# A two-stage attention and mixing kernel: list scheduling by remaining path, one-bank PSUM tiles, and loads gated on earlier loads

## The chip, the cores and the metric

The kernel runs on one core of one Trainium2 chip. The metric is device time in microseconds (us). A core has TensorE (matmuls into the accumulator memory PSUM, which the kernel uses in pieces called banks), VectorE, ScalarE (activation functions by table), GpSimd and SyncE. In the profile they are PE, DVE, ACT, POOL and SP; PEld is TensorE's loading of weights. In this kernel GpSimd issues all loads from HBM (they cast fp32 to bf16 on the way), and SyncE issues the stores, copies of V inside on-chip memory, and transposes done by DMA.

A run more than 1.5% above the fastest of its kernel is called slow; comparisons below use fast runs, each against runs of the kernel before on the same chip.

## The reference, cut to what matters

```python
scores = scale * q @ k.T + bias          # B, H, S, D = 4, 8, 768, 64
# kept: the first 8 positions, and the last 96 up to the query itself
a = softmax(scores);  x = (a @ v)        # heads joined: x is (4, 768, 512)
theta = x @ w_theta                      # 512 x 512
y = w_tok_r @ (x * cos(theta)) + w_tok_i @ (x * sin(theta))    # 768 x 768, over the sequence
u = x + y
out = u + relu(u @ w_ch)                 # 512 x 512
```

Each batch needs all its attention, then theta, then the mix over all positions, so batches overlap: while TensorE mixes one batch, the attention of the next goes in between.

## The kernel before

The kernel is written as a list of operations with a rough duration each. A list scheduler inside the kernel's Python, `Plan`, puts them in an order per engine; the engines then run strictly in that order. So a wrong idea of when data arrives is built into the instruction stream. What the change and the argument touch:

```python
bufs = dict(qk=5, qT=3, kk=3, e=8, x=8, xT=3, ..., w_nat=6, big=2, small=4)   # buffers per pool

def load(fn, nbytes, ndesc, reads=(), writes=(), alloc=None):      # GpSimd issues, in one fixed order
    add(f"load{nload[0]}", {"POOL": 0.62 + 0.00028 * ndesc}, fn, ..., prio=-100 + nload[0],
        lat=(1.5, nbytes / 360e3), after=[previous load])

def load_w_tok(tt):                        # two blocks of 128 rows in one load; 6 loads, 6 buffers
    nc.gpsimd.dma_start(out=w2, in_=src[tt * T:(tt + 2) * T, :].rearrange("(a p) s -> p a s", p=T))

# batches 1 to 3: "vprev", a copy of V shifted by one block, issued by SyncE when V has landed
nc.sync.dma_start(out=dst[NG:T], in_=src[NG:T])
# batches 1 to 3: x transposed by DMA, issued by SyncE too
nc.sync.dma_start_transpose(out=xT, in_=x)
...
big.tile([T, 2, 512], FP)                  # 2 tiles of two PSUM banks: scores of two heads, theta
small.tile(shape, dtype)                   # 4 tiles of one bank: everything else
nc.scalar.activation(e_[:, :, 0:n], tiles[pb][...], AF.Exp, scale=scale)     # both heads at once
...
mix(b, tt, 20 * b + 25, ...)               # priorities are written by hand
```

The softmax here doesn't subtract the row's maximum and nothing guards it: scores larger than these inputs give would overflow.

## Time and profile before

| what | value |
|---|---|
| time, median of 3 | 203.71 us (203.26 to 205.56) |
| span of the profiled run | 200.8 us |
| TensorE busy | 168.4 us, 84% |
| VectorE, ScalarE busy | 124.7, 92.4 us |
| TensorE idle from 70 to 100 us | 16.1 us |
| DMA transpose of x, issue to landing | 8.5 us median, 3.2 at its quickest |

The rows called busy tenths cut the span into 40 slices; a digit is the busy share of a slice in tenths. PEclk is TensorE's granted clock. A line of waits reads: engine, what it was about to write, source line, then what it waited for; total us, times, longest.

### The profile page before, as it was taken

The numbers are of one execution on the slowest core, as the hardware profiler recorded it, in microseconds if no ns is written. First come the engines' busy times: TensorE is split into PE (matmuls) and PEld (weight loads), VectorE is DVE, ScalarE is ACT, GpSimd is POOL, SyncE is SP. The second block draws the span as 40 slices with busy tenths as digits, with TensorE's granted clock in tenths as the row PEclk, the third lists the DMA queues.
The fourth block names the chain that finished last, engine by engine and source line by source line (L and its number), as shares of the span: only waits on it lengthen the run. The fifth ranks groups of instructions, "written<-read, shape, count | busy, mean of one in ns | idle before, by whom it ended". The sixth has DMA issues, their size and how long they took to land.

```text
span 200.8 us, 3765 instructions
## 1 busy us (share of the span) xinstructions
PE 168.4 (84%) x1532; PEld 88.5 (44%) x1532; DVE 124.7 (62%) x243; ACT 92.4 (46%) x100; POOL 69.4 (35%) x85
## 2 busy tenths in 40 slices
PE   7589999899589906804999799999999998999982
PEld 2355466555245502401364355547454653444430
DVE  5475994958496920700397788677988775634351
ACT  2038758899355400600487464187764609400010
POOL 7999745479686855720072000000000000000000
PEclk9859999999999975965899999999999999999998
DMA  5999999999999999999799442832114466124432
GB/s 37 133 147 152 187 210 208 176 154 161 152 184 182 185 138 199 145 148 201 118 102 169 91 131 66 177 100 65 54 30 106 103 148 116 52 52 140 126 104 104
DMA packets 101224, 26.37 MB, mean 131 GB/s; under 512 B 94351, under 2 KB 97055, under 8 KB 101207
## 3 DMA queue, kind: packets, MB, share of 16 engines
q0 software_dynamic: 77568, 12.85, 90.5%
q1 hardware_dynamic: 23639, 13.28, 28.9%
q8 instruction: 12, 0.20, 0.4%
q14 instruction: 5, 0.04, 0.1%
HBM read 25.69 MB, written 6.29 MB: 159 GB/s over the span
## 4 chain that ended last, share of the span: by engine, by line
PE 47%; DMA 33%; POOL 10%; DVE 4%; issue 2%; ACT 1%; SPq 1%; POOLq 0%
PE ps L534 24%; DMA qk<-in_k_dram 11%; PE ps L573 8%; DMA xT<-x 7%; POOL qk L256 6%; PE pb L492 5%; DMA w_nat<-in_moe_w_tok_i_dram 5%; DMA vn<-in_v_dram 5%; DMA out_dram<-o 4%; POOL vn L269 4%; PE pb L448 3%; PE pb L401 3%; DMA uT<-u 2%; PE ps L338 2%; DVE kk L348 1%
## 5 line engine op out<-in xcount | busy, mean ns | idle before, releaser
L534 PE MATMUL ps<-zri,w_tokT 128*128 128x512 bf16 x288 | 70.3, 381 | 0.4 <-ACT w_tokT L327 0.4
L418 ACT ACTIVATE e<-pb 128x1024 bf16<-128x1024 f32 (+1 forms) x48 | 43.9, 951 | 36.3 <-PE pb L401 36.0
L492 PE MATMUL pb<-w_theta_bf,xT 128*128 128x512 bf16 x96 | 25.7, 416 | 16.7 <-DMA xT<-x 16.7
L534 PEld LDWEIGHTS <-w_tokT 128*128 128x128 bf16 x288 | 26.2, 98 | 28.7 <-issue 1.4
L545 DVE TENSOR_TENSOR u<-x,ps 128x512 bf16<-128x512 bf16 x24 | 16.4, 685 | 32.3 <-PE ps L534 32.2
L256 POOL DMA_DIRECT2D qk<-in_q_dram x24 | 21.3, 894 | 25.7 <-PE ps L338 14.7
L426 DVE TENSOR_TENSOR e<-e,etab 128x1024 bf16<-128x1024 bf16 (+1 forms) x36 | 23.0, 642 | 6.7 <-ACT e L418 6.4
L573 PE MATMUL ps<-w_ch_bf,uT 128*128 128x512 bf16 x96 | 24.7, 379 | 1.8 <-DMA uT<-u 1.1
L256 POOL DMA_DIRECT2D qk<-in_k_dram x24 | 21.2, 892 | 5.7 <-DMA qk<-in_q_dram 2.3
L269 POOL DMA_DIRECT2D vn<-in_v_dram x24 | 21.2, 907 | 5.5 <-DMA qk<-in_k_dram 2.0
L492 PEld LDWEIGHTS <-xT 128*128 128x128 bf16 x96 | 9.5, 105 | 30.1 <-DMA xT<-x 18.3
L580 DVE SCALAR_TENSOR_TENSOR o<-ps,u 128x512 f32<-128x512 f32 x24 | 16.6, 690 | 10.0 <-PE ps L573 9.8
L505 ACT ACTIVATE cs<-pb,halfpi 128x1024 bf16<-128x1024 f32 x12 | 13.4, 1114 | 17.5 <-PE pb L492 17.4
L513 DVE TENSOR_TENSOR zri<-x,cs 128x1024 bf16<-128x1024 bf16 x24 | 16.3, 686 | 5.3 <-ACT cs L505 4.8
L338 PE MATMUL ps<-ident,qk 128*128 128x128 bf16 x192 | 15.6, 230 | 4.7 <-DMA qk<-in_q_dram 2.4
L348 DVE COPY kk<-ps 128x2048 bf16<-128x2048 bf16 x12 | 14.5, 1220 | 4.9 <-PE ps L338 4.9
L401 PE MATMUL pb<-qT,kk 64*128 64x128 bf16 x352 | 17.0, 223 | 0.4 <-DVE rec L460 0.4
L401 PEld LDWEIGHTS <-kk 64*128 64x128 bf16 x352 | 10.2, 96 | 14.4 <-issue 12.0
L338 PEld LDWEIGHTS <-qk 128*128 128x128 bf16 x192 | 12.4, 102 | 8.7 <-DMA qk<-in_q_dram 3.4
L505 ACT ACT_TABLE_LOAD x4 | 5.1, 1283 | 23.5 <-PE pb L492 23.5
L448 PEld LDWEIGHTS <-e 128*128 128x128 bf16 x352 | 13.3, 97 | 5.2 <-issue 1.4
L573 PEld LDWEIGHTS <-uT 128*128 128x128 bf16 x96 | 8.5, 98 | 10.8 <-DMA uT<-u 1.7
(53 smaller groups left out, 146.7 us busy)
## 6 DMA issues: line engine op xcount, KB each, us to landing
out_dram<-o SPq DMA_DIRECT2D x24, 256.0 KB, 2.3
qk<-in_q_dram POOLq DMA_DIRECT2D x24, 128.0 KB, 8.3
qk<-in_k_dram POOLq DMA_DIRECT2D x24, 128.0 KB, 8.3
vn<-in_v_dram POOLq DMA_DIRECT2D x24, 128.0 KB, 8.4
vp<-vn SPq DMA_DIRECT2D x9, 243.8 KB, 8.2
w_nat<-in_moe_w_tok_r_dram POOLq DMA_DIRECT2D x3, 384.0 KB, 11.0
w_nat<-in_moe_w_tok_i_dram POOLq DMA_DIRECT2D x3, 384.0 KB, 11.7
w_theta_bf<-in_moe_w_theta_dram POOLq DMA_DIRECT2D x1, 512.0 KB, 6.9
```

The lines of the kernel that those rows point to most:

```text
L256: nc.gpsimd.dma_start(out=tiles["qk", b, g][:, i, t].rearrange("p (h d) -> p h d", d=D), in_=(q, k)[i][b, :, r0:r0 + T, :].rearrange("h p ...
L269: nc.gpsimd.dma_start(out=v_bufs[i][:, t, :, 0:D], in_=v[b, :, r0:r0 + T, :].rearrange("h p d -> p h d"))
L338: nc.tensor.transpose(p_[:, p, t * T:(t + 1) * T], src[:, i, t, p * T:(p + 1) * T], ident)
L401: nc.tensor.matmul(p_[:, hh, s * T:(s + 1) * T], lhsT=tiles["kk", b, kg][R, p, kt, r, :], rhs=tiles["qT", b, g][R, p, qt * T:(qt + 1) * T] ...
L418: nc.scalar.activation(e_[:, :, 0:n], tiles[pb][:, :, 0:n * T].rearrange("p a (s n) -> p a s n", n=T), AF.Exp, scale=scale)
L426: nc.vector.tensor_mul(e_[:, :, 0:n], e_[:, :, 0:n], etab[:, 2 * p:2 * p + 2, s0:s0 + n])
L448: nc.tensor.matmul(o, lhsT=l_, rhs=r_, start=(i == 0), stop=(i == len(mms) - 1))
L492: nc.tensor.matmul(p_[:, t, :], lhsT=tiles["xT", b, g][:, p, t, :], rhs=w_theta_bf[:, p, :], start=(p == 0), stop=(p == NP - 1))
L505: nc.scalar.activation(c_[:, 0], tiles[pb], AF.Sin, bias=halfpi)
L534: nc.tensor.matmul(p_, lhsT=w_tokT[wi][:, 2 * g + t, tt * T:(tt + 1) * T], rhs=tiles["z", b, g][:, wi, t, :], start=(g == 0 and t == 0 and ...
L573: nc.tensor.matmul(p_, lhsT=tiles["uT", b, tt][:, p, :], rhs=w_ch_bf[:, p, :], start=(p == 0), stop=(p == NP - 1))
L580: nc.vector.scalar_tensor_tensor(o_, in0=tiles[ps], scalar=0.0, in1=tiles[uk], op0=ALU.max, op1=ALU.add)
```

## The change

Its intent: let priorities follow from the longest path still ahead, use PSUM in finer pieces, and stop GpSimd's loads of later batches from crowding out SyncE's transfers, by issuing a load only when an earlier one has landed. Cut to its core:

```diff
+    def rank(self):                       # priority: longest remaining path
+        for o in reversed(self.ops):
+            own = min(o.eng.values()) * o.weight
+            tail[o] = own + max((tail[n] + l + ... for n, l in succ.get(o, ())), default=0.0)
...
-    bufs = dict(qk=5, ..., cs=2, ..., w_nat=6, big=2, small=4)
+    bufs = dict(qk=4, ..., cs=3, ..., w_nat=8, pa=4, pb=4)
...
+        if depth:
+            add(f"gate{n}", {"POOL": 0.1},
+                lambda: nc.gpsimd.tensor_copy(out=scrap, in_=landed[n - depth]()),
+                reads=[("ld", n - depth)], prio=-100 + n - 0.5, after=after)
...
-                nc.gpsimd.dma_start(out=w2, in_=src[tt * T:(tt + 2) * T, :]...)      # 6 loads
+                out=new(key, "w_nat", [T, S], BF), in_=src[tt * T:(tt + 1) * T, :])  # 12 loads
...
     for b in range(1, B):
+        depth = 3 if b == 1 else 2
...
-            nc.scalar.activation(e_[:, :, 0:n], tiles[pb][...], AF.Exp, scale=scale)
+            nc.scalar.activation(tiles[ek][:, hh, 0:n], tiles[pb[hh]][:, 0:n], AF.Exp, scale=scale)
...
-            attention(b + 1)
+            plan.weight = 2.0
+            attention(b + 1)
+            plan.weight = 1.0
```

A gate is a copy of one element by GpSimd out of the tile that load n - depth fills. GpSimd works in order, so load n is not issued before that load has landed: at most `depth` loads are in flight. Sines, normalisations and theta are cut to one-bank pieces like the exps; the table of biases for batches 1 to 3 moves to the start. In the profiles of before, `pb` is a two-bank tile and `ps` a one-bank tile; after, `pa` and `pb` are two pools of four one-bank tiles each.

## The prediction

> **What bounds the kernel now.** I read the page first, then the waits, then the chain in order of time, then busy time in stretches of 10 us. The page, sums by engine and the rows of the 40 slices:
>
> ```profile
> PE 168.4 (84%) x1532; PEld 88.5 (44%) x1532; DVE 124.7 (62%) x243; ACT 92.4 (46%) x100; POOL 69.4 (35%) x85
> ...
> PE   7589999899589906804999799999999998999982
> ...
> PEclk9859999999999975965899999999999999999998
> DMA  5999999999999999999799442832114466124432
> ```
>
> TensorE (PE) works 84% of a 200.8 us span, and from slice 21 on it is nearly full. There is one hole, at slices 15 to 20 (some 70 to 100 us), where its clock is cut as well, and a smaller one at slice 11. The DMA engines are near full for as long as loads are issued. The waits name the hole:
>
> ```profile
> PE pb L492 <- DMA xT<-x: 16.7, 4, 8.4
> ...
> POOL qk L256 <- PE ps L338: 14.7, 1, 14.7
> ```
>
> L492 is the theta matmul of batch 1; it waits for xT, a transpose by DMA that SyncE issues. The chain tells why xT is late:
>
> ```profile
> 47.09 7.93 DMA qk<-in_k_dram
> ...
> 69.14 8.52 DMA out_dram<-o
> ...
> 78.63 9.07 DMA vn<-in_v_dram
> ...
> 89.62 8.52 DMA xT<-x
> ...
> 98.18 1.90 PE pb L492 x8
> ...
> 172.43 6.91 PE ps L534 x32
> ```
>
> Every transfer in this stage takes 8 to 9 us, whoever issued it. The xT issue at 89.6 even stands behind copies of V for batch 2 (SyncE issues in order) that waited for a V load to land. The last line is a unit price: 32 matmuls of 512 columns in 6.91 us, 0.216 us each. The stretches:
>
> ```profile
> 50.00:60.00 10.00, 6.62 (x73) 3.55 (x71) 6.88 (x14) 4.36 (x6) 7.51 (x9) 1.00 2.43 169
> ...
> 70.00:80.00 10.00, 2.74 (x7) 1.02 (x8) 1.62 (x4) 0.00 (x0) 5.90 (x7) 0.66 1.87 171
> 80.00:90.00 10.00, 4.62 (x38) 2.27 (x36) 3.85 (x7) 3.31 (x3) 5.26 (x6) 0.84 2.59 148
> 90.00:100.00 10.00, 6.51 (x22) 2.46 (x23) 1.89 (x3) 2.03 (x2) 0.00 (x0) 0.65 1.28 164
> ```
>
> First number: TensorE's busy time in the 10 us. Idle in 70 to 100: 7.26 + 5.38 + 3.49 = 16.1 us. Slow on top of it: eight theta matmuls took 3.59 us at 93.0 and 3.20 us at 77.3, against 1.73 us later, so 3.3 us. At 50 to 60 another 3.4 us go to loads of q and k. The hole is thus worth about 19.5 us. From 100 to 197 TensorE idles only some 3 us.
>
> **What the Trainium skill says.** "DMA: Bandwidth & Descriptors", section "Queues, rings and completion order": each DMA engine goes round the queues that have work, a packet at a time, so GpSimd's and SyncE's transfers slow one another. The trace agrees: xT lands after 8.5 us in the median while loads run and 3.2 us at its quickest; a qk load takes 3.3 us at its quickest (after the pause of 14.7 us) and 8.3 us in the median. "TensorE: Matmul & The Clock Gate", "What's actually happening": an idle window of some 3.4 us halves the clock. It agrees: 0.65 granted in 90 to 100, 0.449 us a matmul against 0.216. "ScalarE: Activation LUTs", "What ACT_TABLE_LOAD costs": an ACTIVATE costs 186 ns + 0.833 ns a column, and neighbours overlap by some 93 ns. The trace has 1022 ns for 1024 columns (formula 1039). For 512 columns I estimate 0.61 us busy, 0.52 from start to start. "PSUM — Partial Sum Buffer", "The four PSUM rules": a matmul's output fits one bank; so a two-bank tile is two matmul groups anyway and can be cut without more matmuls. The built programs agree: as many TensorE instructions in both.
>
> **The change, part by part.**
>
> 1. TensorE's work is unchanged, its order is not. Unit prices from the chain: 512 columns 0.216 us; 24 transposes 1.35 us; 8 score matmuls 0.33; 16 value matmuls 0.48. Per batch: 72 mix, 24 theta, 24 channel matmuls = 120 x 0.216 = 25.9; 48 transposes 2.7; scores 3.7; values 2.7: 35 us. Four batches 140; batch 0's bias matmuls 4.8 (24, about 0.2 each), the other transposes 7, warm-up 3.6: about 155 us if warm and never idle. The 168.4 of before contain 13 us of cold clock and waiting inside groups. Biasing batch 0 on TensorE is nothing new: before had the same 24 bias matmuls.
>
> 2. The exp table (8 x 0.725, some 5.2 us from start to start) moves from 41.8 us, between batch 0 and batch 1, to before the first exp, where ScalarE idles 9.9 us. No table load goes away: 8 in both. Smaller steps: theta in one-bank halves, theta before the transposes of the token weights, those interleaved with the mix. Batch 0's sines should end near 35 us instead of 38.7. But batch 1's q and k cannot arrive sooner, so most of these 4 us turn into a wait for loads.
>
> 3. Gated loads, three in flight for batch 1 and two later. At 3.3 to 3.6 us for a nearly lone load and about 0.3 for gate and semaphore, three in flight give one load per 1.3 us, two give one per 1.9. Before ran one per 1.0 to 1.3. The weights still land near 38 us; batch 1's last k is the 16th load: 39.5 + 15 x 1.3 = 59 us, where before had it at 55.0. So the gate costs 2 to 4 us at the small hole. In return xT, the V copies and stores should land in 3 to 5 us instead of 8.5, and in the new order xT issues no longer queue behind V copies that wait: the hole of 19.5 us shrinks to about 3 (xT of the last group of batch 1: five 0.86 us pieces stand between its values and its theta, against normalise 1 + issue 1.3 + landing 3 to 4).
>
> 4. More small instructions. ScalarE: 32 exps of 1024 columns become 64 of 512, 32 x (2 x 0.61 - 1.022) = +6.3 us; 16 of 768 become 32 of 384 (0.506 each by the same formula), +3.3; 24 cosines and sines become 48 halves, 24 x 0.2 = +4.8; some evacuations (three of q at 1.0, two or three more) leave it, -5. Some 102 us, on an engine with half its time to spare. VectorE: 18 normalisations of two head pairs (0.691 + 0.203) become 36 of one (0.425 + 0.197): 22.4 - 16.1 = +6.3 us; q's evacuations, of which ScalarE did two in batches 2 and 3, go to VectorE almost all: +2. VectorE to about 133 us. Attention of the next batch has double weight, hence is packed tighter: from its first transpose to its last values the new order holds 9.1 us of attention, 11 mix groups and 6 theta or channel groups (17 x 0.863 = 14.7), 23.8 us of TensorE; beside it stand on VectorE 3 k (1.15), 3 q (0.6), 12 multiplications (6.7), 12 normalisations (0.56 each), and nine z, u, o (0.6): 24.7 us. VectorE becomes the tighter engine there, I say 27 us with gaps: +3 us in batch 2 and +3 in batch 3. The 44 matmul groups after batch 3's values are TensorE's alone.
>
> Sum, in span: batch 1's last transpose of k at 59.5. TensorE's work behind it: rest of batch 1's attention 3.3, theta 5.2, rest of mix 0 with channels, and weights 11, mix and channel 1 20.7, batches 2 and 3 70: 110 us, so 169.5 at full pace. Plus 3 (xT), 2 (z behind the last sines of batch 1), 6 (VectorE), 1.5 for the rest; then the end, as before, about 4.5 us from the last mix through u's transposition to the last store. That is 186.5. I take off 3.5, by judgement, because VectorE catches up while TensorE waits for xT or z, so these terms overlap: 183. The time was 1.8 us above the span in the profiled run: **185 us**.
>
> **Rivals.**
>
> A. Two loads in flight starve batches 2 and 3. For: SyncE's transfers keep the engines busy about half the time, and a load that shares takes 4 to 5 us, thus 2.2 to 2.5 us per load; 18 need 40 to 45 us against the 35 us of a batch. Against: a batch's need comes in the middle of its stage, and batch 3 has time. It would cost 5 to 12 us: 190 to 196.
>
> B. VectorE binds throughout attention, with in-order waits, each stage 30 us or longer. For: 24.7 against 23.8 us. Against: it had spare time in every stage of before. 188 to 193.
>
> C. The schedule of the program fits the chip better than I think; no waits for z or xT, loads as early as before. Then 155 us of work, some 10 us of idle start and 5 of end: 172 to 178. For: the new order keeps four or five mix or theta groups between most producers and consumers.
>
> D. The hole stays, since xT still shares with loads and lands in 8 us: 197 to 204. Against: only two or three loads are in flight, where before had five to eight.
>
> **Range and chances.** Most of the 19.5 us must come back unless D holds; A and B take parts of it. A and B together end at 195, C near 177: range 177 to 195. Faster by over 2% (under 199.6): 0.91. Within 2%: 0.07. Slower: 0.02.
>
> **What would show it.** xT's landing in the median at 3 to 5 us; TensorE idle under 10 us in all from 60 us to the last mix, no clock below 0.9 there; busy sum 157 to 162; VectorE 130 to 136; ScalarE 98 to 106; the gates waiting for most of 38 to 130 us on GpSimd; batch 1's last k near 59. Wrong if TensorE waits over 5 us for qk in batch 2 (A), if waits on L462 or on the multiplied e add up to over 10 us (B), or if xT's wait stays over 10 us (D).

## The result, and the profile after

The changed kernel took 223.62 us (median of 3, 221.5 to 223.8). Ratios are the mean time of one kernel's fast runs over that of the other's in the same rounds, so they are not quite the ratio of the medians. Fast were 217.66 and 220.81 us: ratio 1.074, 95% interval 1.05 to 1.098, slower. The profiled run took 221.5 us and counts as slow. What is read from it below, the pace of the loads, is far larger than that 2%, and the gated kernel in experiment 8, profiled in a fast run, shows the same pace.

The page after, sums, rows of slices, and the chain that ended last by engine:

```profile
PE 178.6 (81%) x1532; PEld 94.1 (43%) x1532; DVE 132.8 (60%) x288; ACT 93.9 (43%) x166; POOL 83.9 (38%) x145
...
PE   7598899859475989476299992693999999999992
...
PEclk9859999979979799969859998598599999999999
DMA  6999975999999999999999999999768364333643
...
DMA 48%; PE 25%; POOL 11%; issue 10%; DVE 4%; POOLq 0%; DVEq 0%
```

Before had one hole in the row PE; now there are several, from slice 9 to slice 28, most with a drop of the clock (after the wait of 6.2 us that ends at 139.4, eight matmuls of 512 columns took 3.24 us, 0.405 each against 0.216), and the DMA engines are busy for 28 slices instead of 22. The chain was 47% TensorE and 33% DMA; it is 48% DMA and 25% TensorE, with 11% GpSimd and 10% issue between transfers. Waits after:

```profile
POOL scrap L273 <- DMA qk<-in_q_dram: 20.4, 13, 2.7
...
PE pb L371 <- DMA qk<-in_q_dram: 12.6, 8, 3.6
POOL scrap L273 <- DMA vn<-in_v_dram: 12.4, 11, 3.6
POOL scrap L273 <- DMA qk<-in_k_dram: 12.4, 14, 1.6
PEld L533 <- DMA xT<-x: 11.9, 3, 6.7
PE pa L533 <- DMA xT<-x: 10.7, 2, 6.2
...
POOL w_nat L312 <- PE pb L353: 9.8, 2, 5.8
```

`scrap` is what a gate writes: GpSimd waits 45 us in the gates shown, 49 in all. TensorE waits 12.6 us for q (L371 transposes q and k) and another 4.4 for k, against 2.4 and 1.7 before: it is starved. Its waits for q and k grew by 12.9 us and its busy time by 10.2 (part of that may be the slow run's clock), while its wait for xT fell by 6.0; together 17.1 of the 18.9 us by which the span grew. L312 is a load of token weights that waits for a buffer which TensorE (L353, the transposes of those weights) must free first. TensorE's wait for xT, the hole of before, is still 10.7 us, although xT now lands after 4.4 us in the median. The chain in order of time, a piece of it (start, duration, what):

```profile
84.82 3.63 DMA vn<-in_v_dram
...
88.57 0.18 POOL scrap L273
...
89.02 5.59 DMA qk<-in_q_dram
...
94.73 0.18 POOL scrap L273
...
95.19 3.52 DMA qk<-in_k_dram
```

This pattern makes up most of the chain from 44 to 109 us and again from 115 to 154 us: landing, 0.1 us, gate 0.18 us, 0.3 us, next issue, next landing. From one landing to the next issue it takes 0.57 us (84.82 + 3.63 = 88.45 to 89.02). With two in flight the chain goes through every second load: q, k and V of one group, 5.6 + 3.5 + 3.4 us here, plus three times 0.57, is 14.3 us for six loads, 2.4 us each.

How much TensorE loses is seen in stretches of 10 us, TensorE's busy time first, then the weight loads, VectorE, ScalarE, GpSimd, clock, DMA share and GB/s:

```profile
90.00:100.00 10.00, 5.05 (x29) 2.62 (x28) 2.68 (x6) 1.28 (x3) 4.07 (x8) 0.83 1.21 134
100.00:110.00 10.00, 4.57 (x50) 2.98 (x50) 4.41 (x7) 4.90 (x8) 4.15 (x9) 0.90 1.01 92
...
130.00:140.00 10.00, 3.79 (x24) 1.68 (x23) 3.26 (x7) 1.18 (x2) 3.82 (x8) 0.77 1.46 134
...
150.00:160.00 10.00, 6.39 (x40) 2.90 (x38) 4.41 (x9) 4.25 (x9) 5.08 (x8) 0.66 0.88 68
```

In these 40 us alone it idles 20.2 us. After 160 us, when the last q and k have landed, it is busy to within 0.3 us in every 10 us until the end. And here is why xT is still late, from the timeline:

```profile
86.01 0.42 DVE L503 TENSOR_TENSOR x<-pa,rec 128x256 bf16<-128x256 f32 x1
...
88.50 0.87 SPq L409 DMA_DIRECT2D vp<-vn  x1
...
90.29 1.26 SPq L522 DMA_TRANSPOSE xT<-x  x1
...
95.02 1.46 PE L533 MATMUL pa<-w_theta_bf,xT 128*128 128x512 bf16 x3 [4.50 <-DMA xT<-x]
```

x is complete at 86.4 us. SyncE issues its transpose only at 90.3, because the next instruction in its order is the copy of V for batch 2 (L409), and V landed at 88.45. So the gate holds back a V load, the V load holds back a V copy, the V copy stands before xT in SyncE's queue, and theta of the batch before waits. The longer wait for xT, the 6.2 us until 139.4, has the same form: counting four normalisations to a group, that x was complete at 128.4, the V copy of batch 3 before it in the order went out at 132.8, and the transpose at 133.8.

Issue of the loads, as the timeline of GpSimd has it; a pace is the difference of two starts divided by the 18 loads of a batch (17 for the last batch):

| kernel | first load of batch 1 | batch 2 | batch 3 | last load | pace 1, 2, 3 |
|---|---|---|---|---|---|
| before | 24.6 | 49.9 | 71.3 | 105.9 | 1.41, 1.19, 2.03 |
| changed | 40.7 | 72.7 | 115.5 | 158.7 | 1.78, 2.37, 2.54 |

(Before's last figure holds one wait of 14.7 us for a buffer.)

### The profile page after: what moved, and what is told of

The parts are those of the page before. It is cut to its first block, busy times and chain, and to the rows that moved or that the text cites. A ratio compares the mean times of both kernels' runs of the same rounds, so it can differ in the third digit from the quotient of the medians.

```text
span 219.7 us, 3970 instructions
## 1 busy us (share of the span) xinstructions
PE 178.6 (81%) x1532; PEld 94.1 (43%) x1532; DVE 132.8 (60%) x288; ACT 93.9 (43%) x166; POOL 83.9 (38%) x145
## 4 chain that ended last, share of the span: by engine, by line
DMA 48%; PE 25%; POOL 11%; issue 10%; DVE 4%; POOLq 0%; DVEq 0%
DMA qk<-in_q_dram 15%; DMA qk<-in_k_dram 13%; PE pb L572 13%; DMA vn<-in_v_dram 12%; PE pb L612 7%; POOL qk L286 5%; DMA w_nat<-in_moe_w_tok_r_dram 4%; DMA w_ch_bf<-in_moe_w_ch_dram 3%; POOL vn L300 2%; POOL scrap L273 2%; DMA xT<-x 2%; PE pa L533 2%; PE pa L438 1%; DVE e L469 1%; DVE x L503 1%
## 5 line engine op out<-in xcount | busy, mean ns | idle before, releaser
L572 PE MATMUL pb<-zri,w_tokT 128*128 128x512 bf16 x288 | 74.2, 395 | 2.4 <-DVE zri L554 2.4
L461 ACT ACTIVATE e<-pa 128x512 bf16<-128x512 f32 (+1 forms) x96 | 47.1, 565 | 35.5 <-PE pa L438 35.3
L533 PE MATMUL pa<-w_theta_bf,xT 128*128 128x512 bf16 x96 | 26.2, 408 | 10.8 <-DMA xT<-x 10.7
L371 PE MATMUL pb<-ident,qk 128*128 128x128 bf16 x192 | 18.3, 245 | 17.0 <-DMA qk<-in_q_dram 12.6
L542 ACT ACTIVATE cs<-pa,halfpi 128x512 bf16<-128x512 f32 x24 | 16.6, 691 | 33.7 <-PE pa L533 33.5
L612 PE MATMUL pb<-w_ch_bf,uT 128*128 128x512 bf16 x96 | 27.1, 410 | 0.0
L619 DVE SCALAR_TENSOR_TENSOR o<-pb,u 128x512 f32<-128x512 f32 x24 | 16.4, 688 | 16.4 <-PE pb L612 16.4
L371 PEld LDWEIGHTS <-qk 128*128 128x128 bf16 x192 | 13.5, 109 | 23.0 <-DMA qk<-in_q_dram 15.1
L584 DVE TENSOR_TENSOR u<-x,pb 128x512 bf16<-128x512 bf16 x24 | 16.5, 686 | 7.3 <-PE pb L572 7.2
L438 PE MATMUL pa<-qT,kk 64*128 64x128 bf16 x352 | 18.5, 234 | 1.9 <-ACT e L461 0.7
L438 PEld LDWEIGHTS <-kk 64*128 64x128 bf16 x352 | 11.3, 100 | 15.6 <-issue 10.2
L503 DVE TENSOR_TENSOR x<-pa,rec 128x256 bf16<-128x256 f32 x36 | 15.3, 425 | 1.2
```

The lines of the kernel that those rows point to most:

```text
L371: nc.tensor.transpose(p_[:, t - u0, p], tiles[key][:, i, t, p * T:(p + 1) * T], ident)
L438: nc.tensor.matmul(p_[hh][:, s], lhsT=tiles["kk", b, kg][R, kt, p, r, :], rhs=tiles["qT", b, g][R, qt, p, :], start=not biased, stop=not b ...
L461: nc.scalar.activation(tiles[ek][:, hh, 0:n], tiles[pb[hh]][:, 0:n], AF.Exp, scale=scale)
L503: nc.vector.tensor_mul(xv, po4[:, :, 0:D], rec.to_broadcast([T, 4, D]))
L533: nc.tensor.matmul(p_, lhsT=tiles["xT", b, g][:, p, t, :], rhs=w_theta_bf[:, p, :], start=(p == 0), stop=(p == NP - 1))
L542: nc.scalar.activation(tiles[ck][:, 0], tiles[ps], AF.Sin, bias=halfpi)
```

## The experiments

Theory G: the gates bind, because the gated loads form one chain of landings. With it, W: eight buffers for token weights start that chain late. Rivals: S, the new order and smaller instructions are slower in themselves; I, the gate's instruction costs, not its wait; H, the gates did protect xT and without them the old hole returns. All twelve kernels gave right results. In those made from the changed kernel only GpSimd's stream differs: the schedule was computed as in the changed kernel and only what the gate or the pool emits was altered, and the built programs have the same order on the four other engines.

### 1. No gates

```diff
-                lambda: nc.gpsimd.tensor_copy(out=scrap, in_=landed[n - depth]()),
+                lambda: None,
```

> The changed kernel with the 54 gate copies left out; every other engine's instruction order is the same. Theory G (the gates bind: one load per 1.7 us in batch 1 and 2.4 to 2.5 in batches 2 and 3, where the kernel before ran one per 1.0 to 1.3): batch 1 to 3 loads again come at under 1.5 us each and the time falls below the kernel before, 185 to 200 us. Rival S (the new order and the smaller instructions are slower in themselves): stays above 210 us. Rival H (the gates did protect xT, and without them it lands after 8 us again and the hole of before returns): 200 to 210 us, with TensorE waiting over 10 us for xT.

Measured: 205.82 us (205.43 to 206.75), ratio 1.014 (1.006 to 1.022). The gates cost 6 of the 7.4 per cent. Loads of batches 1 and 2 came at 0.99 and 1.24 us each. S falls as an explanation of the loss. But the time is not below before: it lies where H put it. xT lands after 8.3 us again, though TensorE's wait for it is 5.9 us, not over 10; 6.3 us more go to waits for V copies, and the loads of batch 1 still start at 38.3.

### 2. Gates that wait for nothing

```diff
-                lambda: nc.gpsimd.tensor_copy(out=scrap, in_=landed[n - depth]()),
+                lambda: nc.gpsimd.tensor_copy(out=scrap, in_=zero[0:1, 0:1]),
```

> The changed kernel with each gate copying one element of a constant instead of an element of a landed load: the instruction stays, its wait goes. Theory G (the wait costs, not the instruction): within 3 us of the run without gates, as 0.45 us a gate beside 0.88 us of issue still allows one load per 1.33 us. Rival I (the copy itself costs, through its sharing of GpSimd with the issue of loads): over 210 us.

Measured: 204.9 us, ratio 1.010 (1.001 to 1.018), within 1 us of experiment 1. The 54 copies keep GpSimd busy for 13.2 us in all and cost no time that these runs show. I falls: it is the wait.

### 3. Twelve buffers for the token weights

```diff
-            t_ = sb.tile(shape, dtype, name=pool, tag=pool, bufs=bufs[pool])
+            t_ = sb.tile(shape, dtype, name=pool, tag=pool, bufs=12 if pool == "w_nat" else bufs[pool])
```

> The changed kernel with 12 buffers for the token weights as they are loaded, instead of 8; gates as they are. In the changed kernel GpSimd waits 5.8 and 3.9 us for TensorE to free such a buffer, and everything behind in its queue waits too, so the first load of batch 1 is issued at 40.7 us. Theory G with a late start: the first load of batch 1 is issued some 3 to 5 us earlier and, as the gated chain runs to the end, the time falls by the same 3 to 5 us, to 213 to 219 us. Rival: if the gates were not the chain that ends last, nothing moves (under 1.5 us).

Measured: 214.27 us; fast runs 212.14 and 212.97, ratio 1.047 (1.034 to 1.059). In its profile, of a slow run, the first load of batch 1 starts at 35.5 instead of 40.7, the last of batch 3 at 153.4 instead of 158.7: 5.3 us, carried to the end as a chain carries it. The time fell by some 6 us (ratios 1.074 to 1.047), a little more than expected.

### 4. Both

The two edits together.

> No gates and 12 buffers together. Theory G: 3 to 5 us below the run without gates alone, 182 to 197 us, if loads still bind there; no difference if TensorE binds. Rival S: above 205 us.

Measured: 199.45 us, ratio 0.983 (0.974 to 0.992): the rest of the change is faster than before, by less than G's range said. The two causes add: gates 6.0 to 6.4 per cent, buffers 2.7 to 3.1 (the changed kernel's own ratio is known to 2.4 per cent either way). What is left is in its waits of TensorE, and in xT's landing:

```profile
PE pa L490 <- DMA vp<-vn: 6.4, 2, 3.8
PE pa L533 <- DMA xT<-x: 5.6, 2, 5.3
...
PE pb L371 <- DMA qk<-in_q_dram: 1.2, 2, 0.8
```

Hardly any wait for q, but 12 us for SyncE's V copies (vp) and xT; in the middle of the run (40 to 130 us) xT takes 8.6 us to land in the median, and a V copy issued at 62.3 us landed 9.4 us later. So H holds in part: with nothing gated, loads crowd SyncE's transfers as in the kernel before.

### 5, 6, 7, 10, 11, 12. How many loads in flight

If too few starve TensorE and too many crowd SyncE, some number between should be best. Each is the changed kernel with 12 buffers and another depth for each of batches 1, 2, 3:

```diff
-                lambda: nc.gpsimd.tensor_copy(out=scrap, in_=landed[n - depth]()),
+                lambda: nc.gpsimd.tensor_copy(out=scrap, in_=landed[n - keep[(n - 33) // 18]]()) if keep[(n - 33) // 18] else None,
...
+    keep = (5, 5, 5)    # or (0, 3, 3), (4, 4, 3), (6, 6, 6), (0, 5, 5)
```

Five in flight, first run:

> 12 weight buffers, gates for all of batches 1 to 3 with five loads in flight instead of three and two; same order on every other engine. Theory P (what matters is the pace of the loads against need, so that five in flight, each landing after some 5 to 6 us, give one per 1.1 to 1.3 us, nearly the pace without gates): 195 to 202 us, as without gates, xT landing after 6 to 8 us. Rival (any gate costs by its own wait and instruction): over 205 us.

Batch 1 free, then three:

> 12 weight buffers, batch 1 without gates, batches 2 and 3 with three loads in flight. Theory P: batch 1 comes at full pace (about 1.1 us a load), batch 2 at 1.7 us a load from about 50 us, so it is whole near 82 us, before its need near 92, and meanwhile xT and the V copies of batch 1 land in about 5 us instead of 8 to 9: 189 to 196 us, below the 199.5 of the run without gates. Rival (three in flight are still too slow under SyncE's traffic, 2 us and more a load): 198 to 206 us.

Four, four, three:

> 12 weight buffers, four loads in flight for batches 1 and 2, three for batch 3. Theory P: about 1.35 us a load, batch 1 two to four us later than without gates, transfers of SyncE at 5 to 6 us: 192 to 199 us. Rival: 200 to 207 us.

Six:

> The changed kernel with 12 weight buffers and six loads in flight. Theory P (between five in flight, 193.1, and no gate, 199.5, the time rises as SyncE's transfers slow): 192 to 197 us. Rival (still faster as the pace nears that without gates): under 192 us.

Five again, for an interval:

> The same kernel as the earlier run with five in flight, of whose four times only one counted as fast; run again for an interval. Theory P: 190 to 195 us, 4 to 6% below the kernel before.

Batch 1 free, then five:

> 12 weight buffers, batch 1 without gates, five in flight for batches 2 and 3. Theory P: batch 1 is whole one to three us sooner than with five in flight, and it is what TensorE waits for at 50 to 60 us, so one to three us below that run, 189 to 194 us. Rival: without gates batch 1's loads crowd its own V copies, so no gain or a loss of one to four us.

| in flight in batches 1, 2, 3 | median us | ratio (95%) | pace 1, 2, 3 in us a load |
|---|---|---|---|
| 3, 2, 2 (experiment 3) | 214.27 | 1.047 (1.034 to 1.059) | 1.85, 2.32, 2.52 |
| 4, 4, 3 | 197.23 | 0.969 (0.960 to 0.977) | 1.39, 1.63, 2.00 |
| free, 3, 3 | 194.93 | 0.959 (0.950 to 0.967) | 1.37, 1.79, 1.76 |
| 5, 5, 5 (first) | 193.12 | one fast run only | 1.17, 1.56, 1.34 |
| 5, 5, 5 (again) | 192.11 | 0.950 (0.945 to 0.955) | 1.17, 1.41, 1.47 |
| free, 5, 5 | 193.14 | 0.959 (0.954 to 0.963) | 1.27, 1.44, 1.43 |
| 6, 6, 6 | 194.67 | 0.964 (0.958 to 0.969) | 1.19, 1.40, 1.39 |
| no gates (experiment 4) | 199.45 | 0.983 (0.974 to 0.992) | 1.04, 1.29, 1.94 |

The rows come from three chips, so the ratios are to be compared, each against before on its own chip. Of the depths tried, five is the lowest, 5% below the kernel before, the best version; its interval lies below those of six, of four and of no gates, but overlaps that of "free, 3, 3". For "free, 5, 5" there was no gain over five, as its rival said; the two intervals just touch. The profile of "free, 5, 5", of a fast run, shows what pacing returns when it does not starve; waits of TensorE:

```profile
PE pa L533 <- DMA xT<-x: 3.4, 2, 3.2
...
PE pb L371 <- DMA qk<-in_q_dram: 1.4, 2, 1.1
PE pa L490 <- DMA vp<-vn: 1.2, 1, 1.2
```

6.0 us where experiment 4 has 13.2, and xT lands after 5.6 us (middle of the run, median) instead of 8.6. With six in flight it is 7.3. The two profiles of five throughout, both of slow runs, show it less plainly: there TensorE waits 5.2 and 5.6 us for xT, no less than the 5.6 of experiment 4, with xT landing after 5.0 and 8.1 us; what falls is the wait for V copies, from 6.4 to 0.4 us. Which of SyncE's transfers the gain of pacing comes from is thus not settled.

### 8. The kernel before, gated as the change does it

```diff
+        depth = 0 if n <= 26 else 3 if n <= 44 else 2
+        def fn():
+            if depth:
+                nc.gpsimd.tensor_copy(out=scrap, in_=landed[n - depth]())
+            fn0()
```

> The kernel before with only the gates added, three loads in flight for batch 1 and two for batches 2 and 3; the order on every other engine is that of before. Theory G (the gates starve the kernel whatever its order): batch 2's loads end only near 105 to 110 us, batch 3's near 150: 212 to 226 us. Rival (the gates suit the order of before, whose hole came from crowded transfers): below 200 us, with xT landing after 3 to 5 us and its wait gone.

Measured: 243.76 us, ratio 1.202 (1.193 to 1.211): G, and far worse than its range. The paces are close to those of the changed kernel, 1.70, 2.20, 2.49 us. A wait of TensorE and a piece of SyncE's timeline show where the old order loses 20% to gates that cost the new one 6%:

```profile
PE pb L503 <- DMA xT<-x: 36.0, 3, 18.1
```

```profile
93.87 0.87 SPq L384 DMA_DIRECT2D vp<-vn  x1
...
107.11 0.86 SPq L384 DMA_DIRECT2D vp<-vn  x1
...
108.94 1.27 SPq L492 DMA_TRANSPOSE xT<-x  x1
```

In the old order two V copies of batch 2 stand in a row before one transpose of batch 1, each waiting for its own gated V load, 13 us apart. xT itself lands after 5.3 us; TensorE waits 36 us for it. Against before, TensorE waits 19.3 us more for xT, 6.7 more for q and k and 5.0 more for uT, the transpose of u by DMA, and its busy time grows by 10.2: 41.2 of the 41.4 us.

### 9. The kernel before with five in flight

As experiment 8, with `depth = 0 if n <= 26 else 5`.

> The kernel before with gates of five loads in flight for batches 1 to 3, order as before elsewhere. Theory P+O (pacing helps only together with the new order, in which xT does not stand in SyncE's queue behind V copies that wait for a load): not faster than before, 200 to 212 us, with xT landing sooner but TensorE still waiting over 10 us for it. Rival P alone (the gain of the best version is pacing, which any order would take): 190 to 197 us.

Measured: 209.16 us, ratio 1.038 (1.031 to 1.044). P alone falls: all four runs (208.2 to 210.7) are far from its 190 to 197, and the whole interval lies above 1.02, though the verdict on record is unclear. The pacing that is best in the new order brings the old one no gain. xT lands in 7.0 us (middle of the run, median) where before took 9.0, but batch 1's three transposes are issued at 70.1, 86.8 and 95.7 us, against 67.5, 83.5 and 89.6 before, each right behind V copies, and TensorE waits 17.3 us for xT, against 16.7. So the 5% of the best version come from the new order and the pacing together.

## Why the prediction was wrong

The prediction said 185 us (177 to 195), faster with a chance of 0.91 and slower with 0.02. It is wrong in direction.

- **The step that failed is step 3, "Gated loads".** Its unit price was mis-sized: "At 3.3 to 3.6 us for a nearly lone load and about 0.3 for gate and semaphore, three in flight give one load per 1.3 us, two give one per 1.9." Measured: 0.57 us between landing and next issue; on the chain with two in flight 3.4 to 3.9 us for six of eight k and V loads, but 5.5 to 6.0 for the five q loads issued just after a V copy (3.66 for the one, at 115.5 us, that was not); and so 1.78 us with three and 2.37 and 2.54 with two. I took the quickest landing in the trace, one that was free of traffic, for a load that by design always runs beside SyncE's transfers.
- **Its second error: "The weights still land near 38 us; batch 1's last k is the 16th load: 39.5 + 15 x 1.3 = 59 us".** I priced twelve half-size weight loads as the same bytes and did not count their buffers: 8 for 12, so GpSimd stood 5.8 and 3.9 us, with everything behind it. The last weight landed at 44.6 (37.62 + 7.01). Batch 1's last k was issued at 65.6, and TensorE could transpose it at 70.1, where the sum has 59.5. Experiment 3 gives this about 3 of the 7.4 per cent.
- **Its third: "in the new order xT issues no longer queue behind V copies that wait".** They do, as the timeline at 88.5 us shows; a slower V load makes it worse. I had the order of SyncE before me and looked only at how many V copies precede an xT, not at when the V behind each would land. The hole of 19.5 us was to shrink to about 3; TensorE still waits 10.7 us for xT. So the sign set for rival D, over 10 us, came true without D's reason, as xT lands in 4.4 us.
- **Rival A named the mechanism and was sized too small.** "18 need 40 to 45 us against the 35 us of a batch": 42.7 and 45.7 measured (18 x 2.37, 18 x 2.54). But I gave it "5 to 12 us". The lateness of batch 1, batch 2 and batch 3 adds up along one chain, from 40.7 us to the last q of batch 3, landed at 154.0, and only then TensorE is free to run: 219.7 - 154.0 = 65.7 us to the end. Removing the waits gave 6 per cent, some 12 us, even with xT back at 8 us.
- **Step 1** was right that TensorE's work is the same (1532 matmuls in both). Its estimate of 155 us is not reached as a busy sum: the best versions have 168.7 to 170.5 (for two of the three, 23 of the 1532 matmul records are missing). How much of that is the cold start and how much the end of pipelined matmuls, no run here separates.
- **Step 2** was half right. Batch 0's last sine ends at 37.8 instead of the 35 foretold, against 38.7 before; and TensorE then waits for batch 1's q (1.84 us at 45.5), as said.
- **Step 4** was right on VectorE (132.8 us; said 133), high on ScalarE (93.9; said 98 to 106). Single half exps took 0.600 and 0.495 us, as estimated, but neighbours overlap and a busy sum counts that once: 96 half exps make 47.1 us, where 48 whole ones made 43.9, so +3.2 instead of the +9.6 of step 4. Its list for VectorE beside the attention adds up to 24.1 us, not 24.7. VectorE did not become the bound that was priced at +6 us: in experiment 4, from 110 to 150 us, it is 70 to 93% busy and TensorE idles 1.2 us in all. Rival B falls, and no version comes near the 172 to 178 us of rival C.
- **Rival D** holds in part once the gates go: experiment 4.

What stays open: no run here moved xT ahead of the V copies in SyncE's order, so what that coupling alone costs in the changed kernel is read from its timeline, not tried. Why five in flight is best is not shown by its own two profiles. And the new order, the one-bank tiles and the moved table were tried only together, as what is left in experiment 4.

The idea of the change, that fewer loads in flight let xT land sooner, was right: 4.4 us against 8.5. What it did not buy is time, because a transfer that lands soon but is issued late is still late.

## What to carry to other kernels

When a queue is throttled by "issue when load n - d has landed", price it as a chain: landing time under the traffic that will be there, plus the handover, divided by d; then compare with the pace at which the batches are needed, and look for other queues that wait in order for one of these loads. In this kernel the depth had an optimum between starving and crowding, found by sweeping it: 2 to 3 lost 5%, none gained 2%, five gained 5%, all with the same instruction order on the other engines. When a load is split into more pieces, count the buffers again; an in-order issuer that waits for one buffer holds back all loads behind it.

## What the Trainium skill lacked or had wrong

- "DMA: Bandwidth & Descriptors", "Anatomy of one DMA — SWDGE (gpsimd) path", calls descriptor generation "small, variable". For loads in 1024 pieces GpSimd needed 0.88 us each, 15.8 us for the 18 loads of a batch; for a load of one block of 128 weight rows 0.53.
- The same page's section "Queues, rings and completion order" has the arbitration (the traces agree that transfers of the two queues slow one another; packet by packet no run here shows), but no landing time under load. Measured for a load of 128 KB (as written): 3.2 to 3.6 us nearly alone, 5.5 to 6.0 just after a V copy, 8.3 in the median without gates.
- No page has the pace of dependent issue: from the landing of one load to the issue of the next through a GpSimd copy 0.57 us, 2.4 to 2.5 us a load with two in flight (batches 2 and 3), and in batch 1 1.8 with three, 1.2 with five and 1.0 without a limit.
